# The sign of a float64 weight through a leaky rectifier and a shift, and a new order for the kernel's head

## The chip, the cores and the metric

The kernel runs on one core of a Trainium2 chip. A core has a matrix engine (TensorE, PE in the profile, with its weight loads as PEld), a vector engine (VectorE, DVE), an activation engine (ScalarE, ACT), a general engine (GpSimd, POOL), and a queue engine (SyncE, SP) that here issues all transfers. Each engine takes its instructions strictly in the program's order and waits on semaphores for the others. The metric is the device time of one execution in microseconds (us), median of three runs; lower is better.

## The reference

Three stages follow each other over 4,608 tokens of 512 values (8 batches x 576 positions; 8 heads x 64):

```
q_s = softmax(q, over the 64 of a head);  k_s = softmax(k, over the 576 positions)
x   = q_s @ (k_s^T v)                      # linear attention, heads side by side
g   = silu(x @ w_in);  x2 = g @ w_out      # 512 -> 2048 -> 512
logits = x2 @ phi                          # 32 slots
d = softmax(logits, over tokens);  slots = d^T x2
so = relu(slots @ w1) @ w2, by expert      # 8 experts, 4 slots each
out = softmax(logits, over slots) @ so
```

`w_in` and `w_out` reach the chip as float64, so the kernel must make float32 of their two 32-bit words itself.

## The kernel before, in words

The tokens go through in 18 chunks of 256 (`c`). For a chunk, `qs` is the softmax of q, `qT` its transposition and split into a rounded high part and a rest (`qhi`, `qlo`), `x` the attention product with its own split, `h.c.s` (s = 0 to 7) 24 matmuls with one eighth of `w_in` (`win_hi[s]`, `win_lo[s]`, into one of three PSUM buffers), followed by tanh on ACT, a product on DVE (`u`) and a 32x32 transposition (`gT`). `l`, `dl`, `ds`, `dT` make logits and the running softmax over tokens. `rg` regroups `gT` by 16 transfers into `gk` and `dg` multiplies it with the softmax (the product `sg`). The attention matrices come from 16 units (`u`, half a batch each): `km` maximum, `kT` its transposition, whose maximum `mt` is split (`mh`) and multiplied into a diagonal `dg` tile, `ks` subtraction, `ke` exponential, `kv` matmul and normalisation (`kvtmp`, `kvn_hi`, `kvn_lo`).

No scheduler decides the order. Three strings, START, CHUNK and END, list steps by name; `play` (end of the kernel) runs the next piece of the named generator each time that a name comes up, and every engine gets its instructions in that order. A `*` behind a name puts the step's `combine2` (line 161, a product or a difference of two tiles) on DVE instead of POOL. START makes chunks 0 and 1 and, among them, converts the 16 float64 pieces that the head needs: `w.0` to `w.7` (eighths of `w_in`, each then split into `win_hi` and `win_lo`) and `p.0` to `p.7` (eighths of `w_out`, multiplied with phi into `wphi`). CHUNK, played for chunks 2 to 14, converts `w_out` once more in 16 half pieces (`o`), which are stored to DRAM for the end.

A conversion (`to_f32`) takes, for each piece of 128 x 1024 values: on ACT the high word scaled by 2^-112 (line 384), and the sign of the high word, written over it (line 385); on DVE a left shift by 3 (line 387) and the low word's top bits or-ed in (line 388); on POOL, as a rule, the product with the sign (line 161). The raw words lie in buffers that are loaded again when the piece has been read for the last time, and the raw pieces `p.6` and `p.7` lie in the buffer that `rg.0` writes next. Converted pieces (`mg`) have three buffers.

Of the kernel before, what the change touches and what calls it, by code (L numbers as in the profile page):

```python
# [20 lines left out]


START = """
lq.0 lk.0.0 qs.0 qs.0 qs.0 qs.0 km.0 kT.0 qs.0 kT.0 kT.0 qs.0 lk.1.0 lw.0 km.1 qs.0 ks.0 kT.1 qs.0 w.0 ks.0
qs.0 kT.1 ke.0 qT.0.0 kT.1 lw.1 ks.1 qT.0.0 qT.0.0 w.1 w.0 w.0 ks.1 lphi lk.0.1 lk.1.1 lw.2 kv.0 qT.0.1 ke.1
w.1 w.0 lq.1 kv.1 w.2 qT.0.1 w.1 kv.0 w.0* qs.1 qT.0.1 w.1 kv.0 lw.3 lk.3.0 w.1 w.2 qs.1 lw.4 qs.1 kv.0 kv.1
w.2 kv.1 w.3 kv.1 km.3 kT.3 w.3 x.0.0 qs.1 w.2 x.0.1 x.0.0 w.4 w.3 w.2 x.0.1 kT.3 kT.3* x.0.0 lw.5 qs.1 w.3
w.4 lp.0 w.5 x.0.1 ks.3 qs.1 w.4 h.0.0 ks.3 w.3 w.5 h.0.1 qs.1 w.4 h.0.0 h.0.0 qs.1 w.4* w.5 h.0.2 qs.1 p.0
h.0.1 w.5 lp.1 lk.3.1 p.1 h.0.2 ke.3 lw.6 p.0 h.0.3 w.5 qT.1.0 h.0.1 h.0.4 p.0 lw.7 p.0 p.1 h.0.2 w.6 w.6 p.1
lp.2 qT.1.0 w.7 h.0.4 h.0.3 p.0 w.7 kv.3 p.1 h.0.5 qT.1.0 w.6 p.0 x.1.0 w.6 p.1 qT.1.1 p.1 h.0.3 h.0.4 p.0 p.1  # L30
w.7 kv.3 w.6* h.0.5 qT.1.1 w.7 x.1.0 l.0.1 h.0.6 lk.2.0 p.2 km.2 qT.1.1 x.1.0 p.2 kT.2 w.7 h.0.5 h.0.7 x.1.1
lp.3 p.2 kT.2 kT.2 p.2 kv.3 h.0.6 p.3 h.0.7 x.1.1 p.3 x.1.1 h.0.6 p.2 lp.4 lk.2.1 p.2 h.1.0 ks.2 p.4 lp.5 lq.2
h.0.7 kv.3 p.3 p.3 lp.6 p.4 p.5 p.3 h.1.0 p.4 p.5 h.1.1 p.3 h.1.2 qs.2 p.2 p.4 qs.2 ks.2 p.6 p.4 lp.7 p.3 qs.2
p.5 ke.2 l.0.3 p.4 h.1.0 p.5 h.1.1 p.5 p.7 qs.2 p.6 h.1.3 h.1.2 qs.2 h.1.3 p.6 h.1.1 p.4 p.7 p.5 kv.2 kv.2
p.7* h.1.4 p.6 p.5 qs.2 p.6* h.1.2 p.7 l.0.5 qs.2 p.6 h.1.5 qs.2 qs.2 p.7* kv.2 h.1.4 h.1.3 p.6 rg.0 p.7 h.1.6
p.7 qT.2.0 l.0.7 kv.2 h.1.4 h.1.5 qT.2.0 rg.0 qT.2.0 x.2.0 dl.0 x.2.0 dl.0 qT.2.1 h.1.5 rg.0 qT.2.1 qT.2.1
h.1.7 ds.0 ds.0 x.2.0 ds.0 x.2.1 l.1.1 dT.0 l.1.3 rg.0 x.2.1 h.1.7 h.1.6 dT.0 x.2.1 h.1.6 dg.0 dg.0 h.1.7 lq.3
lk.4.0 lk.4.1 l.1.5
"""
# [24 lines left out]
def kernel(  # L64
# [330 lines left out]
    def conv_w(j):
        yield from to_f32(("w", j), cv_p)
        yield
        t = c_t.pop(("w", j))
# [544 lines left out]
```

## Time and profile before

| | |
|---|---|
| median of three runs (lowest, highest) | 743.89 us (743.63 to 743.97) |
| span of the profiled execution, first to last instruction | 741.5 us |
| busy in that span: PE, DVE, ACT, POOL | 674.9, 569.3, 285.7, 154.2 us |
| mean granted TensorE clock (1 is 2.4 GHz) | 0.970 |

The profile gives the profiled execution's span; the runs' times hold in addition what lies around it, 743.89 - 741.5 = 2.4 us at the median. A busy time is a sum over a program whose stages have different limits, so it is read by stage. A clock of 0.5 in a stretch means 1.2 GHz, 1.0 means 2.4 GHz.

### The profile page before, as it was taken

Reading aid. Unit: us, or ns where it says so; the run is one execution under the profiler, and the core shown is the slowest. Engines: PE = TensorE matmul, PEld = TensorE weight load, DVE = VectorE, ACT = ScalarE, POOL = GpSimd, SP = SyncE. Lnnn points to the kernel's source line nnn. Section 1 sums busy time; section 2 is a strip of 40 time slices with the busy share of each in tenths; the row PEclk is TensorE's granted clock in tenths of the full one; section 3 lists DMA queues with packets and bytes.
Section 4 is the critical chain, followed back from the end, with each engine's and each line's share of the span. In section 5 each row is a group of like instructions: output and inputs, shape, how many; then the busy total and the mean of one; then the engine's idle time right before and its main releaser. Section 6 shows DMA issues by size and latency. Waiting matters only on the chain.

```text
span 741.5 us, 15214 instructions
## 1 busy us (share of the span) xinstructions
PE 674.9 (91%) x6214; PEld 574.7 (77%) x6214; DVE 569.3 (77%) x998; ACT 285.7 (39%) x512; POOL 154.2 (21%) x108
## 2 busy tenths in 40 slices
PE   1347699999999999999999999999999999998993
PEld 1247588889897987989798898989898998893452
DVE  8999999788887979798888778878896784334253
ACT  3466564233444344333434334242433323322223
POOL 4857564011202111122112111010201000003000
PEclk9759799999999999999999999999999999999998
DMA  8623733665565739374765626845351747799998
GB/s 344 276 108 114 304 138 79 187 192 122 161 151 168 199 117 234 99 223 96 204 158 170 143 60 183 264 136 129 102 114 41 217 93 242 265 357 374 369 374 340
DMA packets 39509, 141.73 MB, mean 191 GB/s; under 512 B 6672, under 2 KB 6672, under 8 KB 30736
## 3 DMA queue, kind: packets, MB, share of 16 engines
q1 hardware_dynamic: 39440, 140.76, 60.4%
q8 instruction: 49, 0.80, 0.5%
q14 instruction: 20, 0.16, 0.1%
HBM read 93.55 MB, written 13.63 MB: 145 GB/s over the span
## 4 chain that ended last, share of the span: by engine, by line
PE 71%; DVE 17%; SPq 3%; issue 3%; ACT 2%; DMA 2%; POOL 0%; DVEq 0%; POOLq 0%; ACTq 0%
PE h L432 45%; PE sg L554 5%; PE pl L481 5%; SPq L491 3%; PE l L833 2%; DMA gk<-gT 2%; PE l L806 2%; PE kv L241 2%; DVE mg_p L388 2%; DVE mg_w L388 1%; PE x L348 1%; PE x L349 1%; DVE u L445 1%; PE x L347 1%; PE po L855 1%
## 5 line engine op out<-in xcount | busy, mean ns | idle before, releaser
L432 PE MATMUL h<-x,win_hi 128*128 128x256 f32 x2304 | 432.4, 289 | 5.0 <-DVE u L445 4.1
L432 PEld LDWEIGHTS h<-x,win_hi 128*128 128x128 f32 x2304 | 362.3, 194 | 32.7 <-issue 30.4
L432 PE MATMUL h<-x,win_lo 128*128 128x256 f32 x1152 | 328.1, 285 | 2.0 <-DVE win_lo L161 2.0
L432 PEld LDWEIGHTS h<-x,win_lo 128*128 128x128 f32 x1152 | 222.9, 193 | 2.3 <-DVE win_lo L161 2.3
L443 ACT ACTIVATE u<-h 128x512 f32<-128x512 f32 x144 | 85.5, 596 | 181.6 <-PE h L432 175.7
L445 DVE SCALAR_TENSOR_TENSOR u<-u,h 128x512 f32<-128x512 f32 x144 | 97.1, 674 | 51.0 <-ACT u L443 50.9
L452 DVE STREAM_TRANSPOSE gT<-u 128x512 f32<-128x512 f32 x128 | 91.1, 712 | 4.5
L161 POOL TENSOR_TENSOR q<-q,qsm 128x1024 f32<-128x1024 f32 x16 | 31.6, 1977 | 173.0 <-DVE qsm L303 76.8
L481 PE MATMUL pl<-u,wphi 128*32 128x256 f32 x576 | 47.5, 394 | 2.7 <-DVE wphi L419 2.7
L554 PE MATMUL sg<-gk,d 128*32 128x512 f32 x288 | 40.5, 594 | 1.8 <-DMA gk<-gT 1.4
L354 DVE TENSOR_TENSOR x<-x,x 128x512 fp32r<-128x512 f32 x36 | 24.7, 686 | 22.0 <-ACT x L352 21.5
L161 POOL TENSOR_TENSOR qlo<-q,qhi 128x512 fp32r<-128x512 f32 x17 | 22.5, 1322 | 90.6 <-ACT qhi L329 90.6
L294 ACT ACTIVATE q<-q 128x1024 f32<-128x1024 f32 x18 | 19.1, 1060 | 52.9 <-DVE q L161 48.9
L193 DVE TENSOR_REDUCE m<-kv 128x256 f32<-128x1280 f32 x16 | 39.3, 2454 | 0.0
L352 ACT CAST x<-x 128x512 fp32r<-128x512 f32 x36 | 21.0, 584 | 42.5 <-PE x L349 42.2
L161 POOL TENSOR_TENSOR mg_o<-mg_o,raw_o 128x512 f32<-128x512 f32 x16 | 20.9, 1308 | 73.3 <-DVE mg_o L388 64.8
L257 ACT CAST kvn_hi<-kvtmp 64x128 fp32r<-64x128 f32 x32 | 9.5, 296 | 51.2 <-DVE kvtmp L252 50.8
L329 ACT CAST qhi<-q 128x512 fp32r<-128x512 f32 x34 | 20.9, 615 | 18.9 <-DVE q L323 13.3
L348 PE MATMUL x<-qlo,kvn_hi 128*128 128x256 f32 (+3 forms) x96 | 27.3, 285 | 0.0
L349 PE MATMUL x<-qhi,kvn_lo 128*128 128x256 f32 (+3 forms) x96 | 27.2, 284 | 0.0
L347 PE MATMUL x<-qhi,kvn_hi 128*128 128x256 f32 (+3 forms) x96 | 27.2, 283 | 0.0
L554 PEld LDWEIGHTS sg<-gk,d 128*32 128x32 f32 x288 | 12.1, 109 | 18.7 <-issue 11.8
(155 smaller groups left out, 905.6 us busy)
## 6 DMA issues: line engine op xcount, KB each, us to landing
gk<-gT SPq DMA_DIRECT2D x256, 128.0 KB, 2.5
w<-in_moe_w_dram SPq DMA_DIRECT2D x32, 1024.0 KB, 7.5
kv<-in_kv_dram SPq DMA_DIRECT2D x16, 650.0 KB, 6.2
kv<-in_kv_dram SPq DMA_DIRECT2D x16, 640.0 KB, 4.9
q<-in_q_dram SPq DMA_DIRECT2D x18, 512.0 KB, 3.5
raw_w<-in_moe_w_in_dram SPq DMA_DIRECT2D x8, 1024.0 KB, 7.4
raw_p<-in_moe_w_out_t_dram SPq DMA_DIRECT2D x8, 1024.0 KB, 7.9
raw_o<-in_moe_w_out_dram SPq DMA_DIRECT2D x8, 1024.0 KB, 6.9
```

The lines of the kernel that those rows point to most:

```text
L161: (nc.vector if star[0] else nc.gpsimd).tensor_tensor(*a)
L193: nc.vector.tensor_reduce(m1.rearrange("p (h d) -> p h d", h=HH), k_t[u].rearrange("p h j d -> p h d j"), axis=AX.X, op=ALU.max,)
L347: nc.tensor.matmul(o, kh, qh[:, i, p0:p1], start=True, stop=False)
L348: nc.tensor.matmul(o, kh, ql[:, i, p0:p1], start=False, stop=False)
L349: nc.tensor.matmul(o, kl, qh[:, i, p0:p1], start=False, stop=True)
L354: nc.vector.tensor_tensor(lo, px, hi.bitcast(F32), ALU.subtract)
L432: nc.tensor.matmul(ph[:, i, :], a, x[:, kk, :], start=(n == 0), stop=(n == 3 * KD - 1))
L443: nc.scalar.activation(u, ph, AF.Tanh, scale=0.5)
L445: nc.vector.scalar_tensor_tensor(u, u, 1.0, ph, ALU.add, ALU.mult)
L452: nc.vector.transpose(out=gT_t[c][:, :, 2 * s:2 * s + 2, :].rearrange("p j a f -> p a j f"), in_=u.rearrange("p a (j t) -> p a j t", t=32),)
L481: nc.tensor.matmul(pl_t[c][NS * g:NS * g + NS, :], wphi[:, ft, :], u[:, i, :], start=(ft < G), stop=(ft >= KF - G))
L554: nc.tensor.matmul(pg[NS * i:NS * i + NS, :], d[:, j, :], gk[:, j, i, :], start=(j == 0), stop=(j == TPC - 1))
```

## The change

Sign and product go away. A leaky rectifier (Prelu) passes positive inputs and multiplies negative ones with alpha, here -2^32: the result is positive for both, and for a negative input its exponent is larger by 32, a bit that the left shift by 3 moves to the place of the sign. The piece of a generator that held the product is gone, so each `w`, `p` and `o` has a step less (for `o` two). START is written anew: the loads, conversions and chunk steps of the head come in another order, with other steps marked by `*`. CHUNK only loses two of its six `o`. END is the same.

```
-lq.0 lk.0.0 qs.0 qs.0 qs.0 qs.0 km.0 kT.0 qs.0 kT.0 kT.0 qs.0 lk.1.0 lw.0 km.1 qs.0 ks.0 kT.1 qs.0 w.0 ks.0
+lq.0 lk.0.0 lw.0 lk.1.0 qs.0 qs.0 lk.0.1 lw.2 qs.0 km.0 qs.0 lw.3 w.0 w.0 kT.0 qs.0 qs.0 qs.0 kT.0 qs.0 lw.1
...
-            nc.scalar.activation(mg[:, a], top, AF.Copy, scale=2.0 ** -112)
-            nc.scalar.activation(top, top, AF.Sign)
+            nc.scalar.activation(mg[:, a], top, AF.Prelu, scale=2.0 ** -112, alpha=-2.0 ** 32)
             yield
             nc.vector.tensor_scalar(m, m, 3, None, ALU.logical_shift_left)
             nc.vector.scalar_tensor_tensor(m, w[:, a, :, 0], 29, m, ALU.logical_shift_right, ALU.bitwise_or)
-            yield
-            combine2(mg[:, a], mg[:, a], top, ALU.mult)
             if i < cuts - 1:
                 yield
```

What the new order does is read from the engines' instruction lists. Line numbers behind `to_f32` are four lower after the change, those ahead of it one lower. A number directly behind a tile's name is its piece, unit or chunk; the last number is a buffer's. First POOL in the early head, from the first conversions on, before:

```order
L161 TENSOR_TENSOR qlo0_0_244<-qt0_0_245,qhi0_0_243 128x512
L161 TENSOR_TENSOR mg_w0_232<-mg_w0_232,raw_w0_218 128x1024
L161 TENSOR_TENSOR mg_w1_258<-mg_w1_258,raw_w0_218 128x1024
L161 TENSOR_TENSOR qlo0_1_292<-qt0_1_293,qhi0_1_291 128x512
L161 TENSOR_TENSOR win_lo1_151<-mg_w1_258,win_hi1_143 128x1024
L161 TENSOR_TENSOR mg_w2_322<-mg_w2_322,raw_w2_268 128x1024
L161 TENSOR_TENSOR q1_299<-q1_299,qmx1_333 128x1024
L161 TENSOR_TENSOR mg_w3_360<-mg_w3_360,raw_w2_268 128x1024
L161 TENSOR_TENSOR win_lo2_152<-mg_w2_322,win_hi2_144 128x1024
L161 TENSOR_TENSOR mg_w4_391<-mg_w4_391,raw_w4_347 128x1024
L161 TENSOR_TENSOR win_lo3_153<-mg_w3_360,win_hi3_145 128x1024
```

and after, up to the last `win_lo`:

```order
L160 TENSOR_TENSOR win_lo0_150<-mg_w0_208,win_hi0_142 128x1024
L160 TENSOR_TENSOR qlo0_1_267<-qt0_1_268,qhi0_1_266 128x512
L160 TENSOR_TENSOR win_lo2_152<-mg_w2_235,win_hi2_144 128x1024
L160 TENSOR_TENSOR q1_306<-q1_306,qmx1_308 128x1024
L160 TENSOR_TENSOR win_lo4_154<-mg_w4_424,win_hi4_146 128x1024
L160 TENSOR_TENSOR q1_306<-q1_306,qsm1_493 128x1024
L160 TENSOR_TENSOR win_lo5_155<-mg_w5_427,win_hi5_147 128x1024
L160 TENSOR_TENSOR qlo1_0_542<-q1_306,qhi1_0_541 128x512
L160 TENSOR_TENSOR win_lo6_156<-mg_w6_545,win_hi6_148 128x1024
```

The products `mg_w...<-mg_w...,raw_w...` are gone, and from POOL's list up to the `dg2` tile six `win_lo` differences stand there instead of five, and one `qlo` less. Next DVE, from the maximum of unit 3 to the second half of chunk 0's x, before:

```order
L193 TENSOR_REDUCE m1_3_365<-kv3_340 128x256
L387 TENSOR_SCALAR mg_w3_360<-mg_w3_360 128x1024
L388 SCALAR_TENSOR_TENSOR mg_w3_360<-raw_w2_268,mg_w3_360 128x1024
L207 TENSOR_REDUCE mt3_397<-m1T_10_367 128x2
L209 CAST mh3_399<-mt3_397 128x2
L210 TENSOR_TENSOR mt3_397<-mt3_397,mh3_399 128x2
L161 TENSOR_TENSOR dg3_402<-ident_74,mh3_399 128x128 x2
L161 TENSOR_TENSOR dg3_402<-ident_74,mt3_397 128x128 x2
L354 TENSOR_TENSOR x1_0_373<-x_11_374,x0_0_372 128x512
L387 TENSOR_SCALAR mg_w4_391<-mg_w4_391 128x1024
L388 SCALAR_TENSOR_TENSOR mg_w4_391<-raw_w4_347,mg_w4_391 128x1024
L354 TENSOR_TENSOR x1_0_373<-x_12_383,x0_0_372 128x512
```

and after:

```order
L192 TENSOR_REDUCE m1_3_349<-kv3_311 128x256
L353 TENSOR_TENSOR x1_0_352<-x_10_353,x0_0_351 128x512
L206 TENSOR_REDUCE mt3_372<-m1T_11_365 128x2
L208 CAST mh3_374<-mt3_372 128x2
L209 TENSOR_TENSOR mt3_372<-mt3_372,mh3_374 128x2
L259 TENSOR_TENSOR kvn_lo0_160<-kvtmp1_346,kvn_hi0_158 64x2x64 x2
L385 TENSOR_SCALAR mg_w3_362<-mg_w3_362 128x1024
L386 SCALAR_TENSOR_TENSOR mg_w3_362<-raw_w2_201,mg_w3_362 128x1024
L353 TENSOR_TENSOR x1_0_352<-x_12_387,x0_0_351 128x512
L160 TENSOR_TENSOR win_lo1_151<-mg_w1_247,win_hi1_143 128x1024
L160 TENSOR_TENSOR win_lo3_153<-mg_w3_362,win_hi3_145 128x1024
L160 TENSOR_TENSOR dg3_430<-ident_74,mh3_374 128x128 x2
```

Before, five conversions (`mg_w0` to `mg_w4`) and the `dg3` tile stand ahead of the second x1_0 row; now four conversions do, and `dg3`, `mg_w4` and two `win_lo` follow it. `win_lo0`, which stood further ahead on DVE, is on POOL now. Last DVE, at the end of the conversions, before (`mg_p6`, then `mg_p7` with its product on DVE):

```order
L387 TENSOR_SCALAR mg_p6_955<-mg_p6_955 128x1024
L388 SCALAR_TENSOR_TENSOR mg_p6_955<-raw_p6_877,mg_p6_955 128x1024
L445 SCALAR_TENSOR_TENSOR u1_1_980<-u1_1_980,h1_1_891 128x512
L452 STREAM_TRANSPOSE gT1_973<-u1_1_980 128x2x8x32
L419 TENSOR_SCALAR wphi_87<-wphi_30_969 128x64
L387 TENSOR_SCALAR mg_p7_984<-mg_p7_984 128x1024
L388 SCALAR_TENSOR_TENSOR mg_p7_984<-raw_p6_877,mg_p7_984 128x1024
L249 TENSOR_SCALAR rz2_1050<-kv_33_1029 128x2
L250 RECIPROCAL rz2_1050<-rz2_1050 128x2
L252 TENSOR_TENSOR kvtmp2_1053<-kv_33_1029,rz2_1050 128x128
L161 TENSOR_TENSOR mg_p7_984<-mg_p7_984,raw_p6_877 128x1024
```

and after, where `mg_p7` comes first and `mg_p6` later:

```order
L385 TENSOR_SCALAR mg_p7_983<-mg_p7_983 128x1024
L386 SCALAR_TENSOR_TENSOR mg_p7_983<-raw_p6_793,mg_p7_983 128x1024
L296 TENSOR_REDUCE qsm2_989<-q2_789 128x32
L224 TENSOR_TENSOR kv2_683<-kv2_683,mb_29_977 128x5x4x64
L248 TENSOR_SCALAR rz3_996<-kv_16_595 128x2
L249 RECIPROCAL rz3_996<-rz3_996 128x2
L251 TENSOR_TENSOR kvtmp3_999<-kv_16_595,rz3_996 128x128
L385 TENSOR_SCALAR mg_p6_909<-mg_p6_909 128x1024
L386 SCALAR_TENSOR_TENSOR mg_p6_909<-raw_p6_793,mg_p6_909 128x1024
L301 SCALAR_TENSOR_TENSOR qsm2_989<-qsm2_989,qsm_31_1029 128x32
L302 RECIPROCAL qsm2_989<-qsm2_989 128x32
L415 TENSOR_SCALAR wphi_87<-wphi_30_1026 128x64
```

Behind `mg_p6` DVE goes on with the q product of chunk 2 (`q2_789<-q2_789,qsm2_989`, on POOL before), a fifth u of chunk 1, a `qlo` of chunk 2 and the second `kvn_lo` of batch 1. Up to that `kvn_lo` (unit 2's, the last that x of chunk 2 needs) DVE's list holds, before: `win_lo0`, `win_lo4`, `win_lo6` and the product of `mg_p7`, and 12 u; after: `win_lo1`, `win_lo3`, the q product, two `qlo`, and 13 u. All else up to there is the same work in another order. On ACT the whole program has one load of the function tables before and one after; in the head after, the 16 Prelu stand in nine groups between instructions that use Exp or Tanh.

## Rows read from the trace of the kernel before

**Rows 1.** Busy us by engine in four stretches, with clock, DMA share and GB/s.

```profile
0.00:49.81 49.81, 13.16 (x110) 10.73 (x111) 44.90 (x68) 24.76 (x28) 31.02 (x30) 0.82 0.68 271
49.81:88.89 39.08, 28.33 (x228) 25.31 (x227) 38.60 (x38) 24.02 (x30) 28.08 (x12) 0.81 0.42 158
88.89:140.64 51.75, 50.74 (x459) 43.72 (x459) 45.51 (x70) 25.07 (x37) 21.80 (x13) 0.96 0.49 157
140.64:640.00 499.36, 495.78 (x4596) 440.20 (x4596) 402.51 (x740) 182.26 (x349) 65.99 (x46) 1.00 0.57 155
```

**Rows 2.** DVE's groups up to 128.3 us: busy us, mean ns | idle before.

```profile
L388 DVE SCALAR_TENSOR_TENSOR mg_w<-raw_w,mg_w 128x1024 uint32<-128x1024 uint32 x8 | 15.0, 1872 | 0.3
L388 DVE SCALAR_TENSOR_TENSOR mg_p<-raw_p,mg_p 128x1024 uint32<-128x1024 uint32 x8 | 14.0, 1754 | 0.3
L387 DVE TENSOR_SCALAR mg_p<-mg_p 128x1024 uint32<-128x1024 uint32 x8 | 9.6, 1203 | 0.0
L452 DVE STREAM_TRANSPOSE gT<-u 128x512 f32<-128x512 f32 x12 | 8.5, 711 | 0.5
L387 DVE TENSOR_SCALAR mg_w<-mg_w 128x1024 uint32<-128x1024 uint32 x8 | 9.1, 1140 | 0.0
L161 DVE TENSOR_TENSOR win_lo<-mg_w,win_hi 128x1024 fp32r<-128x1024 f32 x3 | 8.4, 2804 | 0.0
L445 DVE SCALAR_TENSOR_TENSOR u<-u,h 128x512 f32<-128x512 f32 x12 | 8.0, 667 | 0.0
L209 DVE CAST mh<-mt 128x2 fp32r<-128x2 f32 x4 | 3.7, 916 | 0.1
L161 DVE TENSOR_TENSOR mg_p<-mg_p,raw_p 128x1024 f32<-128x1024 f32 x1 | 1.2, 1215 | 0.0
```

**Rows 3.** DVE's instructions in order of time: start us, us, engine, line, what.

```profile
11.10 0.17 DVE L209 CAST mh<-mt 128x2 fp32r<-128x2 f32 x1
...
44.07 2.20 DVE L209 CAST mh<-mt 128x2 fp32r<-128x2 f32 x1
46.31 2.27 DVE L210 TENSOR_TENSOR mt<-mt,mh 128x2 f32<-128x2 f32 x1
...
91.65 0.68 DVE L387 TENSOR_SCALAR mg_p<-mg_p 128x1024 uint32<-128x1024 uint32 x1
92.37 1.22 DVE L388 SCALAR_TENSOR_TENSOR mg_p<-raw_p,mg_p 128x1024 uint32<-128x1024 uint32 x1
...
127.71 0.56 DVE L260 TENSOR_TENSOR kvn_lo<-kvtmp,kvn_hi 64x128 fp32r<-64x128 f32 x2
```

**Rows 4.** POOL's instructions in order of time, around 45 us.

```profile
43.84 2.41 POOL L161 TENSOR_TENSOR mg_w<-mg_w,raw_w 128x1024 f32<-128x1024 f32 x1 [4.88 <-issue]
46.20 2.35 POOL L161 TENSOR_TENSOR win_lo<-mg_w,win_hi 128x1024 fp32r<-128x1024 f32 x1
```

**Rows 5.** POOL's groups up to 128.3 us.

```profile
L161 POOL TENSOR_TENSOR mg_w<-mg_w,raw_w 128x1024 f32<-128x1024 f32 x8 | 19.6, 2456 | 16.0 <-issue 6.1 <-DVE mg_w L388 4.5 <-ACT raw_w L385 3.4
L161 POOL TENSOR_TENSOR mg_p<-mg_p,raw_p 128x1024 f32<-128x1024 f32 x7 | 17.3, 2478 | 15.3 <-issue 7.9 <-DVE mg_p L388 4.6 <-ACT u L443 2.8
L161 POOL TENSOR_TENSOR win_lo<-mg_w,win_hi 128x1024 fp32r<-128x1024 f32 x5 | 12.8, 2559 | 0.0
```

**Rows 6.** ACT's groups up to 128.3 us.

```profile
L384 ACT ACTIVATE mg_w<-raw_w 128x1024 f32<-128x1024 f32 x8 | 9.2, 1155 | 5.4 <-issue 4.8 <-POOL win_lo L161 0.5
L294 ACT ACT_TABLE_LOAD x1 | 1.3, 1283 | 4.3 <-DMA q<-in_q_dram 4.3
```

**Rows 7.** The chain that ended last, around 135 us: start us, us, what.

```profile
130.43 0.23 PE x L347
...
140.64 4.39 PE h L432 x35
```

**Rows 8.** PE's instructions in order of time: the first of h.

```profile
49.81 0.81 PE L432 MATMUL h<-x,win_hi 128*128 128x256 f32 x2
```

**Rows 9.** SP's instructions in order of time: chunk 0's regrouping.

```profile
121.23 10.43 SPq L491 DMA_DIRECT2D gk<-gT  x16
```

More of the change, by code (lines that the diff above doesn't have):

```diff
@@ L23 @@
 START = """
-lq.0 lk.0.0 qs.0 qs.0 qs.0 qs.0 km.0 kT.0 qs.0 kT.0 kT.0 qs.0 lk.1.0 lw.0 km.1 qs.0 ks.0 kT.1 qs.0 w.0 ks.0
[L25 to L38, printed above, removed]
+lq.0 lk.0.0 lw.0 lk.1.0 qs.0 qs.0 lk.0.1 lw.2 qs.0 km.0 qs.0 lw.3 w.0 w.0 kT.0 qs.0 qs.0 qs.0 kT.0 qs.0 lw.1
@@ new lines @@
+km.1 kT.0 w.2 ks.0 kT.1 qs.0 lphi w.2 w.1 kT.1 w.0 lk.1.1 ks.0 kT.1 qT.0.0 qT.0.1 ke.0 ks.1 qT.0.0 ks.1 ke.1
+kv.0 w.1 kv.0 w.0 lq.1 qs.1 qT.0.1 lk.3.0 kv.1 qs.1 lw.4 kv.0 kv.0 qT.0.0* kv.1 qs.1 km.3 x.0.0 w.2 x.0.0 w.3
+x.0.0 kT.3 kv.1 qT.0.1 w.2 kT.3 kv.1 qs.1 lk.3.1 lw.5 lp.0 w.3 lp.1 x.0.1 x.0.1 x.0.1 w.1 w.1* w.3 h.0.0 w.4
+w.3* w.5 qs.1 kT.3* h.0.0 w.4 h.0.1 p.0 w.5 h.0.2 qs.1 h.0.1 qs.1 qs.1 h.0.0 lw.6 w.4 w.4 h.0.1 w.5 qs.1 w.5
+ks.3 h.0.3 qT.1.0 ks.3 w.6 p.0 h.0.4 p.1 p.1 lw.7 h.0.4 w.6 ke.3 p.0 h.0.3 h.0.2 p.0 kv.3 qT.1.0 h.0.2 w.7 lp.2
@@ new lines @@
+w.6 p.1 qT.1.0 w.7 w.6 p.0 p.1 w.7 h.0.5 h.0.3 h.0.4 h.0.5 x.1.0 x.1.0 p.1 lk.2.0 w.7 h.0.6 qT.1.1 p.2 h.0.7
+qT.1.1 km.2 h.0.6 lp.3 p.3 lp.4 x.1.0 p.0 qT.1.1 x.1.1 p.2 p.1 h.0.5 lp.5 x.1.1 x.1.1 p.3 p.2 h.0.6 p.2 p.5 p.4
+l.0.1 lq.2 h.0.7 lp.6 kT.2 h.1.0 h.0.7 p.5 h.1.2 p.4 h.1.1 h.1.0 kT.2 p.3 p.2 p.4 h.1.1 qs.2 p.3 p.2 lp.7 h.1.2
+p.6 p.3 h.1.0 qs.2 qs.2 kT.2 h.1.1 h.1.3 h.1.6 ks.2 h.1.2 p.3 p.7 qs.2 qs.2 p.7 qs.2 ks.2 h.1.6 p.4 kv.3 h.1.4
+p.4 qs.2 lk.2.1 ke.2 p.6 qs.2 l.0.3 p.5 h.1.4 p.4 p.5 kv.3 p.6 p.7 qs.2* p.5 p.6* h.1.4 kv.2 kv.3 p.6 rg.0 p.6
@@ L39 @@
+rg.0 h.1.3 p.7* h.1.5 qT.2.0 lk.4.0 kv.2 rg.0 p.5 p.7 kv.2 l.0.5 qT.2.0 h.1.3 qT.2.0* p.7 lk.4.1 l.0.7 kv.2 dl.0
+dl.0 x.2.0 x.2.0 qT.2.1 ds.0 ds.0 qT.2.1 h.1.7 qT.2.1 x.2.1 ds.0 h.1.6 x.2.0 dT.0 h.1.5 l.1.1 dT.0 x.2.1 h.1.5
+h.1.7 l.1.3 h.1.7 l.1.5 rg.0 x.2.1 dg.0 lq.3 dg.0
 """
 CHUNK = """
-qs rg km h.0 h.0 o h.1 qs e.7 rg h.1 dl kT o h.0 kT sc sc kT* dl qs qs* h.1 h.2 rg ks ds h.3 ks ds qs h.2 h.3
-ds sc ke h.4 dT qs sc h.2 dT qs ol qs h.3 rg kv l.1 dg kv o sc qs qT.0 h.5 kv ow qT.0 h.4 kv qT.0* h.4 x.0 h.5
@@ L43 @@
-o qT.1 h.5 qT.1 x.0 qT.1 l.3 h.6 x.1 h.7 l.5 lk dg x.0 o x.1 h.6 x.1 h.6 o h.7 h.7 lq
+qs rg km h.0 h.0 o h.1 qs e.7 rg h.1 dl kT o h.0 kT sc sc kT* dl qs qs* h.1 h.2 rg ks ds h.3 ks ds qs h.2 h.3 ds
+sc ke h.4 dT qs sc h.2 dT qs ol qs h.3 rg kv l.1 dg kv sc qs qT.0 h.5 kv ow qT.0 h.4 kv qT.0* h.4 x.0 h.5 o qT.1
+h.5 qT.1 x.0 qT.1 l.3 h.6 x.1 h.7 l.5 lk dg x.0 o x.1 h.6 x.1 h.6 h.7 h.7 lq
 """
```

## The prediction

> **What bounds the kernel now.** I read the busy time by stretch first [rows 1]. From 140.64 to 640 us PE is busy 495.78 of 499.36 us at full clock: there the matmuls bound the kernel, and what DVE, ACT or POOL save is hidden. The head is another matter. In its first two stretches PE is busy 13.16 of 49.81 us and 28.33 of 39.08 us at clocks of 0.82 and 0.81, while DVE is busy 44.90 and 38.60 us, nearly without a gap. From 88.89 to 140.64 us PE is busy 50.74 of 51.75 us. So DVE bounds the kernel up to about 89 us, and PE then works off what DVE has delivered late. ACT (about half busy) and POOL bound nothing by themselves.
>
> The second view is DVE's own time. A conversion's or-instruction takes 1.22 us when nothing disturbs it and its shift 0.68 us [rows 3], but their means up to 128 us are 1.75 to 1.87 and 1.14 to 1.20 us [rows 2]. Why, two pairs show: a cast of 128 x 2 values takes 0.17 us at 11.10 us and 2.20 us at 44.07 us, and the tiny subtraction behind it 2.27 us [rows 3]. Each ends within 0.05 us of a POOL instruction, a sign product (43.84 + 2.41) and a `win_lo` difference (46.20 + 2.35) [rows 4]. DVE stands still until POOL's instruction is over, and the profile counts that as busy.
>
> These stalls, summed over the groups of [rows 2] as mean minus undisturbed time: or-instructions 8 x 0.65 + 8 x 0.53 = 9.5 us, shifts 8 x 0.46 + 8 x 0.52 = 7.9 us, three `win_lo` on DVE 3 x (2.80 - 1.22) = 4.8 us, four casts 4 x (0.92 - 0.17) = 3.0 us: 25.2 us of the first 128. They are the cover under which this head is slow.
>
> **The change, part by part.** *Sign on ACT.* Sixteen instructions fall away in the head and sixteen shorter ones in the chunk loop, in the head about the size of the copy that stays, 1.16 us [rows 6], so some 18 us of ACT. ACT is half busy and not on the chain; I cost this at nothing. Cover: DVE's list in the head, PE in the loop. Prelu itself stands in no row. Nearest is the scaled copy of the same tile, 1.16 us; the other end is that each change of function costs a table load of 1.28 us more [rows 6]. I take the copy's price, since the program has one load as before; the other end is a rival below.
>
> *Products on POOL.* Fifteen go from the head, 19.6 + 17.3 = 36.9 us of POOL's 80.9 us up to 140.6 us [rows 1, 5]. POOL's own time is off the path; what counts is the stalls that they cause on DVE. The sixteenth stood on DVE (1.22 us [rows 2]). In the chunk loop sixteen shorter products go, under PE's cover: worth nothing, or at most part of the 3.6 us that PE idles there [rows 1]. If that cover were gone, DVE would be stalled there the same way.
>
> *The new order, on DVE.* The last thing that x of chunk 2 waits for is the `kvn_lo` of unit 2, which ends at 127.71 + 0.56 = 128.3 us [rows 3]. Ahead of it after the change: one u more (0.67 + 0.71), two `win_lo` (2 x 1.22), the q product (1.22, the same size), two `qlo` of half that size (estimate 2 x 0.61); in all 6.3 us. No longer ahead of it: three `win_lo` and a product, 4 x 1.22 = 4.9 us [rows 2]. Net +1.4 us.
>
> *The stalls that stay.* POOL keeps 80.9 - 36.9 = 44 us, less a little, in it six `win_lo` of 2.4 to 2.6 us [rows 4, 5]. Before, 80.9 us of POOL cost DVE 25.2 us, 0.31 us each us; at that rate 44 us cost 13.6. The lower end is 3 us (a `win_lo` or two that meet a conversion), the upper 44 us (each blocks DVE for all its length). I take 7 us, half the rate: in the new list the last four `win_lo` and the `qlo` meet DVE mostly at u, transpositions and reductions, whose means, 0.67 us for u and 0.71 for gT, show no such stretching [rows 2].
>
> *New waits.* With the stalls gone DVE meets others that are not ready. Its list puts the sum behind unit q1 ahead of u0_0, and that sum's matmul stands on PE behind h0_2; ACT does u0_2 only behind u0_4, kv3 and u0_3, so h0_5 waits for its PSUM buffer. Before, DVE's gaps in the head are small (49.81 - 44.90 = 4.9 us, then 0.5 [rows 1]). Bounds for more: 0 and 9 us (three h of about 3 us); I take 3.
>
> *The sum.* 128.3 - 25.2 + 1.4 + 7 + 3 = 114.5 us for that `kvn_lo`. From x of chunk 2 to the first h of chunk 2 PE took 140.64 - 130.43 = 10.2 us [rows 7], the same matmuls after the change. So h of chunk 2 starts at 124.8 us instead of 140.64: 15.8 us earlier. From there the program is the same and bound by PE. The span goes from 741.5 to 725.7 us, and the time, with the 2.4 us around it, to 743.9 - 15.8 = **728 us**.
>
> *Can PE keep up?* h starts at 49.81 us [rows 8]. Ahead of it on DVE go at least the two stalls of [rows 4] (4.1 us), one conversion (1.9), and a `win_lo` with its stall (2.8): 8.8 us. From 49.81 to 140.64 us PE idles 10.75 + 1.01 = 11.8 us [rows 1]. Without both, and at the same clocks, h of chunk 2 could start at 140.6 - 8.8 - 11.8 = 120 us. That is a floor close under 124.8; less time at 1.2 GHz would lower it by a few us.
>
> **The rule on the port.** The row: DVE's 0.17 us cast takes 2.20 us and ends with POOL's product [rows 3, 4]. The Trainium skill, page "SBUF — State Buffer", section "Who interferes with whom", says that DVE and GpSimd share a port pair as an exclusive lock: the second to start blocks until the first has finished, if DVE's instruction is of a fast two-port kind or reads two SBUF operands. The trace agrees as far as the pairs show. Taken at its strictest, for every POOL instruction that is left, it gives the second rival.
>
> **Rivals.**
> *New waits take most of it.* The order is tight: u, PSUM buffers, regrouping. Chunk 0's regrouping is the clearest place: its 16 transfers were issued from 121.23 us for 10.43 us [rows 9], when piece p.7 was done, and now wait for the late p.6, about 6 us ahead of the `kvn_lo`, at 108 us; their last lands near 121, just ahead of the products that need it. If DVE waits 9 us and the rate of 13.6 us holds, the `kvn_lo` ends at 127 and the time is 741; half of that again would leave no change. For it: DVE becomes one of three nearly equal chains. Against: PE's floor is 120.
>
> *Slower: what is left on POOL blocks DVE fully.* Place: the six `win_lo`, the q differences and `qlo`, on DVE's list. Price: up to 44 us instead of 7, time up to 743.9 - 15.8 + 37 = 765. It decides from 23 us of stalls. Against: 81 us of POOL cost only 25.
>
> *Slower: Prelu is of another table.* Nine groups of Prelu among Exp and Tanh would mean 18 loads of 1.28 us, 23 us on ACT; if all lie on the path, 751 us; it turns slower from 13 of them. The Trainium skill, page "ScalarE: Activation LUTs", section "Table sets: the hidden batching unit", names relu and copy among the functions that every set has, not Prelu; no run here shows it. Against: the program loads once.
>
> *Larger gain.* Stalls of 3 us, no waits, and a clock that rises earlier: 119 us or less for h of chunk 2, time 717 to 722.
>
> **How the numbers follow.** My forecast (stalls and waits between 4 and 17 us together, 722 to 735): 0.72. New waits: 0.12, of it 0.09 for 735 to 742 and 0.03 for no change. Full blocking 0.04, tables 0.02. Larger gain 0.10. The range is 717 to 738: it takes in the larger gain and the first part of the new waits, and leaves out some 0.13 above. Within 0.2% (1.5 us) is about what a measurement of this kernel can't tell from no change; faster has 0.72 + 0.09 + 0.10 = 0.91, same 0.03, slower 0.06.
>
> **What would show it.** Right: `mg` shifts and or-instructions near 0.68 and 1.22 us on DVE, long ones only beside `win_lo` or q instructions on POOL; the first h near 40 us; h of chunk 2 near 125; from there the same distance to the end; Prelu near 1.16 us and one table load. Wrong: or-instructions that still take 1.8 us; gaps on DVE that name PE, ACT or a transfer for over 10 us together; PE idle in front of the products `sg` of chunk 0; more idle time on PE in the loop than 3.6 us.

## The result and the profile after

The changed kernel takes **714.0 us** (median of 4 runs, 712.8 to 716.5) beside 743.9 for the kernel before, measured along with it: a ratio of 0.960, 95% interval 0.957 to 0.963. It gained 29.9 us where I had forecast 15.8, and it lies 3 us below my range. The profiled execution took 714.5 us, its span 712.7.

The busy time by stretch, to be read beside [rows 1] (columns: stretch, length, then busy us of PE, weight loads, DVE, ACT and POOL, clock, DMA share, GB/s; the cuts are just behind the first h at 35.06 us, at 65 us, and just behind the start of h of chunk 2 at 114.62 us):

```profile
0.00:35.26 35.26, 13.41 (x109) 10.34 (x110) 31.40 (x64) 13.80 (x17) 18.28 (x25) 0.94 0.83 326
35.26:65.00 29.74, 27.16 (x247) 25.48 (x246) 28.45 (x37) 21.73 (x28) 14.53 (x7) 0.95 0.66 250
65.00:114.69 49.69, 47.71 (x443) 40.01 (x441) 41.04 (x77) 19.25 (x34) 5.07 (x7) 0.97 0.57 178
114.69:612.00 497.31, 496.01 (x4604) 441.33 (x4605) 404.82 (x739) 171.89 (x333) 45.05 (x30) 1.00 0.58 157
```

The first h starts at 35.1 us instead of 49.8 [rows 8], h of chunk 2 at 114.6 instead of 140.6, and from 35.26 us up to there PE is busy 74.9 of 79.4 us. Behind it PE is busy 496.0 of 497.3 us, so the chunk loop is bound by PE as before. So 26 of the 30 us were won in the head.

DVE's groups up to the end of the last `kvn_lo` of unit 2, now at 102.8 us (mean ns behind the comma; the first five groups answer to lines of [rows 2]):

```profile
L386 DVE SCALAR_TENSOR_TENSOR mg_w<-raw_w,mg_w 128x1024 uint32<-128x1024 uint32 x8 | 9.8, 1226 | 0.3
L386 DVE SCALAR_TENSOR_TENSOR mg_p<-raw_p,mg_p 128x1024 uint32<-128x1024 uint32 x8 | 9.8, 1225 | 0.3
L385 DVE TENSOR_SCALAR mg_w<-mg_w 128x1024 uint32<-128x1024 uint32 x8 | 6.5, 809 | 0.9 <-ACT mg_w L383 0.9
L385 DVE TENSOR_SCALAR mg_p<-mg_p 128x1024 uint32<-128x1024 uint32 x8 | 5.4, 676 | 0.0
L208 DVE CAST mh<-mt 128x2 fp32r<-128x2 f32 x4 | 0.7, 169 | 0.1
L209 DVE TENSOR_TENSOR mt<-mt,mh 128x2 f32<-128x2 f32 x4 | 0.6, 160 | 0.1
L259 DVE TENSOR_TENSOR kvn_lo<-kvtmp,kvn_hi 64x128 fp32r<-64x128 f32 x8 | 2.2, 277 | 0.1
L192 DVE TENSOR_REDUCE m<-kv 128x256 f32<-128x1280 f32 x4 | 9.5, 2381 | 0.0
```

None of these is stretched any more, except two shifts by 0.5 us each (they make the mean 809). Yet POOL keeps six `win_lo` of 2.4 to 3.4 us. Where they went, two lists in order of time show, POOL and then DVE:

```profile
28.18 2.76 POOL L160 TENSOR_TENSOR win_lo<-mg_w,win_hi 128x1024 fp32r<-128x1024 f32 x1 [1.26 <-ACT win_hi L395]
...
48.29 2.42 POOL L160 TENSOR_TENSOR win_lo<-mg_w,win_hi 128x1024 fp32r<-128x1024 f32 x1
```

```profile
29.39 2.41 DVE L192 TENSOR_REDUCE m<-kv 128x256 f32<-128x1280 f32 x1
...
47.98 0.71 DVE L448 STREAM_TRANSPOSE gT<-u 128x512 f32<-128x512 f32 x1
48.62 0.67 DVE L322 STREAM_TRANSPOSE q<-q 128x512 f32<-128x512 f32 x1
49.21 1.45 DVE L224 TENSOR_TENSOR kv<-kv,mb 128x1280 f32<-128x1280 f32 x1
```

Beside a `win_lo` DVE now works on a maximum, on transpositions, or on something that it reads from PSUM (`mb`, `h`), and these keep their times: the transposition of u 0.71 us as in the kernel before [rows 2], the maximum 2.38 us in the mean, where before it took 2.36:

```profile
L193 DVE TENSOR_REDUCE m<-kv 128x256 f32<-128x1280 f32 x4 | 9.4, 2362 | 0.0
```

On PE, x of chunk 2 starts where that `kvn_lo` ends, and the regrouped pieces of chunk 0 are the last thing waited for ahead of h of chunk 2:

```profile
102.91 0.30 PE L346 MATMUL x<-qhi,kvn_hi 128*128 128x64 f32 x1
...
112.81 1.88 PE L550 MATMUL sg<-gk,d 128*32 128x512 f32 x10 [0.76 <-DMA gk<-gT]
114.62 0.50 PE L428 MATMUL h<-x,win_hi 128*128 128x256 f32 x2
```

Prelu takes the time of the scaled copy [rows 6], and one table is loaded, at 0.7 us:

```profile
L383 ACT ACT_TABLE_LOAD x1 | 1.3, 1283 | 0.7 <-PEq L928 0.7
...
L383 ACT ACTIVATE mg_w<-raw_w 128x1024 f32<-128x1024 f32 x8 | 9.1, 1155 | 18.0 <-DMA raw_w<-in_moe_w_in_dram 18.0
```

### The profile page after: what moved, and what is told of

Read it like the earlier page. It is cut to its first block, busy times and chain, and to the rows that moved or that the text cites. A ratio compares the mean times of both kernels' runs of the same rounds, so it can differ in the third digit from the quotient of the medians.

```text
span 712.7 us, 15115 instructions
## 1 busy us (share of the span) xinstructions
PE 671.3 (94%) x6214; PEld 572.1 (80%) x6214; DVE 543.0 (76%) x999; ACT 256.0 (36%) x480; POOL 90.2 (13%) x75
## 4 chain that ended last, share of the span: by engine, by line
PE 78%; DVE 9%; DMA 5%; SPq 3%; ACT 2%; issue 2%; DVEq 0%; ACTq 0%
PE h L428 51%; PE sg L550 5%; PE pl L477 5%; SPq L487 3%; DMA gk<-gT 2%; PE l L829 2%; PE kv L240 2%; PE l L802 2%; PE po L851 2%; DMA raw_p<-in_moe_w_out_t_dram 2%; PE x L348 1%; PE x L347 1%; PE x L346 1%; PE uT L461 1%; DMA raw_w<-in_moe_w_in_dram 1%
## 5 line engine op out<-in xcount | busy, mean ns | idle before, releaser
L160 POOL TENSOR_TENSOR q<-q,qsm 128x1024 f32<-128x1024 f32 x15 | 28.7, 1914 | 259.9 <-DVE qsm L302 188.2
L477 PE MATMUL pl<-u,wphi 128*32 128x256 f32 x576 | 46.0, 390 | 0.3 <-DVE wphi L415 0.3
L160 POOL TENSOR_TENSOR qlo<-q,qhi 128x512 fp32r<-128x512 f32 x16 | 20.7, 1296 | 105.1 <-ACT qhi L328 105.1
L240 PE MATMUL kv<-kv 128*64 128x65 f32 x640 | 24.0, 235 | 3.3 <-ACT kv L231 3.3
L550 PEld LDWEIGHTS sg<-gk,d 128*32 128x32 f32 x288 | 11.8, 109 | 18.7 <-issue 13.0
L322 DVE STREAM_TRANSPOSE q<-q 128x512 f32<-128x512 f32 x34 | 23.5, 692 | 3.8 <-POOL q L160 3.8
```

What stands on the lines that cost most here:

```text
L240: nc.tensor.matmul(pk[D * e:D * e + D, i, :], kt[:, 2 * i + e, j, :], va[:, 2 * i + e, j, :], start=(j == 0), stop=(j == KJ - 1),)
L477: nc.tensor.matmul(pl_t[c][NS * g:NS * g + NS, :], wphi[:, ft, :], u[:, i, :], start=(ft < G), stop=(ft >= KF - G))
L550: nc.tensor.matmul(pg[NS * i:NS * i + NS, :], d[:, j, :], gk[:, j, i, :], start=(j == 0), stop=(j == TPC - 1))
```

## The experiments

Theory A: DVE's stalls beside POOL's work made the head slow; without products, and with the rest of POOL's work placed beside DVE work that it doesn't stall, they are gone. Theory B: the new order, with its earlier loads, brings the time, whatever POOL does. Theory C: the arithmetic alone brings it.

For each run I summed the **stalls**: DVE's conversions, casts, `mt`, `win_lo`, `kvn_lo` and q steps up to the last `kvn_lo` of unit 2, each one's duration less its undisturbed one (or-instruction 1.22 us, shift 0.68, cast 0.17, `mt` 0.16, `win_lo` 1.22, `kvn_lo` 0.28, q product 1.22, `qlo` 0.69); and DVE's **waits** there, as the trace names them. Ratios are to the kernel before, measured along with each. The time is a median; the last four columns are of the one run that was profiled, whose time stands ahead of them and can lie some us from the median.

| kernel | time us | ratio (95%) | profiled run us | first h | stalls | waits | last `kvn_lo` ends |
|---|---|---|---|---|---|---|---|
| before | 743.9 | 1 | 743.9 | 49.8 | 29.9 | 4.9 | 128.3 |
| changed | 714.0 | 0.960 (0.957 to 0.963) | 714.5 | 35.1 | 1.1 | 7.0 | 102.8 |
| arithmetic alone | 730.6 | 0.983 (0.981 to 0.986) | 727.8 | 43.1 | 14.1 | 8.9 | 115.2 |
| order alone | 746.3 | 1.006 (1.003 to 1.008) | 746.1 | 41.1 | 24.8 | 15.1 | 135.9 |
| idle products | 734.8 | 0.988 (0.985 to 0.991) | 730.6 | 39.7 | 18.7 | 6.7 | 120.8 |
| idle copies | 726.1 | 0.977 (0.974 to 0.979) | 725.7 | 39.9 | 11.6 | 5.3 | 112.9 |
| Sign kept | 720.6 | 0.971 (0.968 to 0.973) | 723.1 | 36.1 | 2.2 | 11.2 | 109.4 |
| arithmetic alone, Sign kept | 730.6 | 0.984 (0.981 to 0.988) | 730.2 | 45.0 | 14.2 | 9.7 | 117.0 |
| loop as before | 714.2 | 0.962 (0.959 to 0.964) | 715.1 | 34.9 | 1.0 | 4.9 | 101.3 |
| no or-instructions | 708.5 | 0.953 (0.950 to 0.956) | 708.2 | 34.8 | 0.5 | 21.9 | 98.8 |

### The two parts of the change

Arithmetic alone (the old lists without the product steps):

```diff
-            nc.scalar.activation(mg[:, a], top, AF.Copy, scale=2.0 ** -112)
-            nc.scalar.activation(top, top, AF.Sign)
+            nc.scalar.activation(mg[:, a], top, AF.Prelu, scale=2.0 ** -112, alpha=-2.0 ** 32)
...
-            yield
-            combine2(mg[:, a], mg[:, a], top, ALU.mult)
```

> The rectifier and the shift carry the sign, but all steps stay in the order of before; the product steps are dropped from it. Theory A (DVE loses its time standing still beside POOL's two-input instructions; the products are half of them, and the new order keeps the rest away from DVE's SBUF work): the stalls that win_lo causes stay, those of the products go, so about half to two thirds of the 30 us gained: 722 to 729 us, mean of the or-instruction on DVE up to the end of the head between 1.3 and 1.6 us. Theory B (the new order, with earlier loads and another sequence, brings it; the arithmetic only shortens ACT and POOL, which bound nothing): 738 to 744 us. Theory C (the arithmetic alone brings it all, the order nothing): 713 to 717 us.

Order alone (the new lists; the product follows in the step of the or-instruction):

```diff
             nc.vector.scalar_tensor_tensor(m, w[:, a, :, 0], 29, m, ALU.logical_shift_right, ALU.bitwise_or)
-            yield
             combine2(mg[:, a], mg[:, a], top, ALU.mult)
```

> The new order with the arithmetic of before (scaled copy, Sign, and the product on POOL right behind the or-instruction). Theory A: fifteen products of 2.4 us are back beside DVE, so the or-instructions and shifts are long again, 15 to 25 us of stalls: 728 to 742 us. Theory B: 714 to 720 us, since POOL and ACT have room. Theory C: 738 us or more, the order alone gives nothing.

730.6 and 746.3 us: neither part does it, and their effects (by the ratios some 13 us gained and some 4 lost) don't add up to 29.9. Theories B and C are out. Theory A's own ranges were missed as well, 722 to 729 by 1.6 us and 728 to 742 by 4.3; the marks that it named came, or-instructions of 1.49 us with the arithmetic alone (1.3 to 1.6 expected) and stalls of 24.8 us with the order alone (15 to 25). DVE's conversions with the arithmetic alone, up to 115.2 us:

```profile
L387 DVE SCALAR_TENSOR_TENSOR mg_p<-raw_p,mg_p 128x1024 uint32<-128x1024 uint32 x8 | 12.0, 1496 | 0.3
L387 DVE SCALAR_TENSOR_TENSOR mg_w<-raw_w,mg_w 128x1024 uint32<-128x1024 uint32 x8 | 11.9, 1490 | 0.3
L386 DVE TENSOR_SCALAR mg_w<-mg_w 128x1024 uint32<-128x1024 uint32 x8 | 9.2, 1154 | 0.0
```

Two groups with the order alone, up to 135.9 us:

```profile
L387 DVE SCALAR_TENSOR_TENSOR mg_w<-raw_w,mg_w 128x1024 uint32<-128x1024 uint32 x8 | 15.0, 1870 | 0.3
L208 DVE CAST mh<-mt 128x2 fp32r<-128x2 f32 x4 | 5.4, 1357 | 0.1
```

Without products the old order keeps 14.1 us of stalls, from `win_lo` and q steps that meet conversions. With products the new order keeps 24.8 us, and DVE waits 15.1 us besides, so that it is slower than before. Together they leave 1.1 us.

### Does POOL's work itself do it?

Into the changed kernel I put one more POOL instruction behind each of the head's sixteen conversions. It writes to the logits' tile, which is free then. First a product, then a copy:

```diff
+            if key[0] != "o":
+                spare = logit[:, 0:32, :].rearrange("p (a t) s -> p a (t s)", a=n)
+                nc.gpsimd.tensor_tensor(spare, mg[:, a], mg[:, a], ALU.mult)
```

> The changed kernel, with one 128x1024 product more on POOL behind each of the sixteen conversions of the head; it reads the converted piece twice and writes into the logits' tile, which is free then, and nobody waits for its values. It leaves nothing of the computation out. Theory A (POOL's two-input work itself stalls DVE): 8 to 20 us slower than the changed kernel, 722 to 734 us, with or-instructions and shifts of 1.4 us or more in the mean. Theory B (the products cost by the chain conversion, product, win_hi, and by the order): 714 to 718 us, means near 1.23 and 0.75 us; some of it could come from win_lo, which queue behind the products on POOL.

```diff
-                nc.gpsimd.tensor_tensor(spare, mg[:, a], mg[:, a], ALU.mult)
+                nc.gpsimd.tensor_copy(spare, mg[:, a])
```

> As the run with idle products (734.8 us), but the sixteen instructions on POOL are copies of the same 128x1024 tiles, one input instead of two. If any work of POOL on SBUF stalls DVE: 728 to 736 us, or-instructions near 1.75 us again. If what stalls DVE is an instruction with two inputs: 714 to 719 us and or-instructions near 1.23 us; some of it could then be win_lo and q steps that queue behind the copies.

The products cost 20.8 us, above my bound of 20, and stalls rise by 17.6. The copies cost 12.1 us, with 10.5 us more of stalls; their 726.1 us lie in neither of the two ranges, so the guess that only two inputs on POOL count fell, and so did the one that any instruction there costs the same. A tiny cast, beside a product and beside a copy (DVE and POOL in order of time):

```profile
95.23 1.89 POOL L389 TENSOR_TENSOR logit<-mg_p 128x1024 f32<-128x1024 f32 x1 [1.23 <-DVE mg_p L386]
95.46 1.69 DVE L208 CAST mh<-mt 128x2 fp32r<-128x2 f32 x1
```

```profile
88.90 1.04 POOL L389 COPY logit<-mg_p 128x1024 f32<-128x1024 f32 x1 [1.20 <-DVE mg_p L386]
89.14 0.83 DVE L208 CAST mh<-mt 128x2 fp32r<-128x2 f32 x1
```

Each time the 0.17 us cast ends with POOL's instruction: the shorter instruction costs less, no more. The or-instructions' mean was 1.74 us with products and 1.40 with copies, the shifts' 0.79 and 0.83, where I had expected 1.4 or more for both with products. Part of either cost is that `win_lo` and the q steps queue behind the added instruction and then meet conversions.

### Sign and the chunk loop

Sign put back on ACT, its values unused, in the changed kernel and in the old order with the new arithmetic:

```diff
             nc.scalar.activation(mg[:, a], top, AF.Prelu, scale=2.0 ** -112, alpha=-2.0 ** 32)
+            nc.scalar.activation(top, top, AF.Sign)
```

> The changed kernel, with the Sign activation of before put back on ACT behind each rectifier, its values used by nobody: ACT works as long as before. If ACT's time is free, as I costed it: 714 to 716 us. Rival (part of the gain that I did not forecast comes from a shorter ACT, which delivers u and win_hi earlier): 718 to 724 us, with DVE waits that name ACT for 4 us or more in the head.

> The kernel with the rectifier in the order of before (arith alone, 730.6 us), with the Sign put back on ACT, its values used by nobody. If ACT is free in that order, as it looked in the profile of before: 729 to 732 us, and the 13 us that the arithmetic alone gained are all the products'. If ACT's time counts there as it did in the new order (6 to 7 us there): 735 to 740 us, and only some 6 us are the products'.

In the old order it costs nothing that can be told: 730.6 us with and without it. In the new one it costs 6.6 us (720.6; by the two ratios, 8). The stretch from 35 to 65 us, of the changed kernel and then with Sign (columns as in the first view):

```profile
35.00:65.00 30.00, 27.41 (x248) 25.74 (x247) 28.71 (x37) 21.73 (x28) 14.53 (x7) 0.95 0.66 252
```

```profile
35.00:65.00 30.00, 24.80 (x195) 22.81 (x196) 25.50 (x34) 25.03 (x29) 8.66 (x5) 0.78 0.56 211
```

ACT is busy 25.0 of 30 us, and DVE 3.2 us less than without Sign. PE's clock has a mean of 0.78 instead of 0.95: from 55 to 60 us PE is busy 1.3 of 5 us (5.0 without Sign), and from 60 to 65 us the clock is 0.50, that is 1.2 GHz (1.00 without). DVE's waits that name ACT come to 4.9 us up to the last `kvn_lo`, 2.5 in the changed kernel. The longest of DVE's waits with Sign (us in total, times, longest), and POOL's list:

```profile
DVE x L353 <- ACT x L351: 2.7, 2, 2.4
DVE q L322 <- POOL q L160: 2.5, 1, 2.5
DVE u L442 <- ACT u L440: 1.4, 1, 1.4
```

```profile
48.55 2.41 POOL L160 TENSOR_TENSOR win_lo<-mg_w,win_hi 128x1024 fp32r<-128x1024 f32 x1 [14.68 <-ACT win_hi L396]
50.92 1.92 POOL L160 TENSOR_TENSOR q<-q,qsm 128x1024 f32<-128x1024 f32 x1
```

ACT's late `win_hi` holds POOL; the q product behind it starts at 50.9 us, and in the changed kernel at 46.4:

```profile
46.42 1.91 POOL L160 TENSOR_TENSOR q<-q,qsm 128x1024 f32<-128x1024 f32 x1
```

DVE waits 2.5 us for it.

In the chunk loop, the conversion and list of before (head as changed):

```diff
+            if key[0] == "o":
+                nc.scalar.activation(mg[:, a], top, AF.Copy, scale=2.0 ** -112)
+                nc.scalar.activation(top, top, AF.Sign)
...
+                combine2(mg[:, a], mg[:, a], top, ALU.mult)
```

> The changed kernel, but the sixteen half pieces of w_out in the chunk loop are converted as before, with Sign and product, and the loop's list is that of before; the head is that of the change. Theory A (the products and Signs of the loop, which I costed at nothing, held the chunk loop up by some 3 us): 716 to 719 us, and the time from the first sg to the end of the span 2 us or more longer. Theory B (PE covers them, as forecast; the loop's few us come from elsewhere, such as late transfers): 713 to 715.5 us, the same distance within 1 us.

714.2 us, ratio 0.962 (0.959 to 0.964): by the time, the loop's products and Signs cost nothing that can be told. The second mark, though, fell on theory A's side: from the first `sg` to the end of the span it took 604.3 us, 2.2 more than in the changed kernel (602.1). This distance varies: it is 604.2 with Sign kept, and over all fourteen profiles 599.9 to 604.3. So a cost of up to some 2 us in the loop isn't excluded.

### What bounds the changed kernel

> The changed kernel without the sixteen or-instructions of the head (it leaves out the low three bits of each mantissa of w and p), to see what bounds the changed kernel now: 16 x 1.23 = 19.6 us less on DVE, 3.7 us of it ahead of the first h. If DVE's list still sets the end of the head alone: the last kvn_lo near 84 us and a time near 695 us. If PE does from the first h on (27.2 of 29.7 and 47.7 of 49.7 us busy): only the three or-instructions ahead of the first h and the 4.6 us of idle PE behind it can be had, 705 to 710 us. If transfers or ACT do: 711 to 714 us.

```diff
-            nc.vector.scalar_tensor_tensor(m, w[:, a, :, 0], 29, m, ALU.logical_shift_right, ALU.bitwise_or)
+            if key[0] == "o":
+                nc.vector.scalar_tensor_tensor(m, w[:, a, :, 0], 29, m, ALU.logical_shift_right, ALU.bitwise_or)
```

This kernel leaves out the low three mantissa bits of w and p. 19.6 us less on DVE bring 5.5 us (708.5): DVE now waits 21.9 us, and PE is full:

```profile
65.00:90.00 25.00, 25.00 (x229) 23.05 (x231) 17.51 (x34) 11.54 (x16) 3.39 (x5) 1.00 0.59 198
```

So, behind the first h, the changed head is within some 6 us of what PE allows. Four tries to start h earlier found nothing. The zeros of the kvn tiles on ACT:

```diff
-        nc.gpsimd.memset(t.bitcast(F32), 0.0)
+        for i in range(NPAIR):
+            nc.scalar.activation(t[:, i, :], ident, AF.Copy, scale=0.0)
```

> The changed kernel with the zeros of the four kvn tiles written by ACT (sixteen scaled copies of 128x128 by 0, while ACT waits for its first piece of w) instead of four memsets on POOL, beside which DVE's first copies stand still for up to 1.7 us. If those stalls are POOL's: the copies of the set-up end at 3.8 to 4.0 us in place of 4.4 to 5.3, and 712 to 714 us, at most 1.5 us better, about what the measurement can tell. If DVE then waits for the first q or for ACT: no difference, 713 to 716 us.

The maximum over the K of unit 3 behind x of chunk 0, in two ways, and the second with those zeros too (the lists' places):

```diff
-kv.0 w.1 kv.0 w.0 lq.1 qs.1 qT.0.1 lk.3.0 kv.1 qs.1 lw.4 kv.0 kv.0 qT.0.0* kv.1 qs.1 km.3 x.0.0 w.2 x.0.0 w.3
-x.0.0 kT.3 kv.1 qT.0.1 w.2 kT.3 kv.1 qs.1 lk.3.1 lw.5 lp.0 w.3 lp.1 x.0.1 x.0.1 x.0.1 w.1 w.1* w.3 h.0.0 w.4
+kv.0 w.1 kv.0 w.0 lq.1 qs.1 qT.0.1 lk.3.0 kv.1 qs.1 lw.4 kv.0 kv.0 qT.0.0* kv.1 qs.1 x.0.0 x.0.0 kv.1 w.2
+x.0.0 qT.0.1 w.2 kv.1 qs.1 w.3 km.3 kT.3 lk.3.1 lw.5 lp.0 x.0.1 x.0.1 x.0.1 w.3 kT.3 lp.1 w.1 w.1* w.3 h.0.0 w.4
...
+x.0.0 kv.1 qT.0.1 w.2 kv.1 qs.1 lk.3.1 lw.5 lp.0 w.3 lp.1 x.0.1 x.0.1 x.0.1 km.3 w.1 w.1* w.3 h.0.0 kT.3 w.4
```

> The changed kernel with another order at one place: the 2.4 us maximum over the K of unit 3 and what follows it, which stand on DVE ahead of the last kvn_lo and x of chunk 0, go behind them, and two conversions of w with them. If the first h of chunk 0 (35.06 us) sets what comes after, since PE is busy 27.2 of 29.7 us from there on: the first h 1.5 to 2.5 us earlier and 711 to 713 us. If the DVE list up to 103 us sets it, whatever the order in it: 713 to 716 us, no difference.

> The maximum over the K of unit 3 moved again, since in the run before (716.2 us) its transposition stood on PE ahead of x of chunk 0 and made it wait 4.4 us: now the maximum goes behind x of chunk 0 on DVE and its transposition behind the first h on PE. If the first h sets what follows: the first h 1.5 to 2.5 us earlier, near 33 us, and 711 to 713 us. If what is lost by the late unit 3 or by ACT takes it back: 713.5 to 716 us.

> The same order, and the zeros of the kvn tiles written by ACT: the set-up ends 0.7 to 1.6 us earlier. If both gains come through to the first h: near 32.5 us and 710 to 712.5 us. If the head is held elsewhere: 713 to 716 us.

713.8, 716.2, 716.6 and 716.0 us, with ratios from 0.959 to 0.964: none can be told from the change, and 716.2 and 716.6 lie just above both of their ranges. The first h came at 34.7, 35.6, 34.4 and 34.5 us. The zeros on ACT did end the set-up at 3.9 us in place of 5.5 (or 4.7), but the first h came only 0.4 us earlier than in the changed kernel. In the first of the two orders my edit left the maximum's transposition on PE ahead of x, which waited 4.4 us for it. In the second the maximum no longer lay beside POOL's `win_lo` and the q step behind it, and something that stalls did (POOL, then DVE):

```profile
28.24 2.75 POOL L160 TENSOR_TENSOR win_lo<-mg_w,win_hi 128x1024 fp32r<-128x1024 f32 x1 [1.26 <-ACT win_hi L395]
30.95 1.91 POOL L160 TENSOR_TENSOR q<-q,qmx 128x1024 f32<-128x1024 f32 x1
```

```profile
31.55 1.78 DVE L259 TENSOR_TENSOR kvn_lo<-kvtmp,kvn_hi 64x128 fp32r<-64x128 f32 x2 [0.52 <-ACT kvn_hi L256]
```

The two `kvn_lo` that take 0.6 us undisturbed took 1.8: in the changed kernel the 2.4 us maximum covers them.

## Why the prediction was wrong

The forecast of 728 us is 14 us above the measured time. Some 10 of them lie ahead of h of chunk 2 (124.8 us forecast, 114.6 measured), 4 behind it.

**The mechanism was right.** DVE's stalls beside POOL's work were the head's cost, the products were what to remove, and the time is gained ahead of h of chunk 2. Products that nobody needs bring the stalls back. But without the products the old order gains only 13 of the 30 us; the new order, whose effect on the stalls I had put at half the rate, is what takes the rest of POOL's work out of DVE's way.

**The step that failed** is "The stalls that stay": 7 us, measured 1.1. I took half of a mean rate per us of POOL. There is no such rate: what a `win_lo` costs depends on which DVE instruction is due beside it, and I could have read that from the new list. Without the products POOL is busy 41.0 us up to the last `kvn_lo` in the old order and 36.6 in the new one; DVE's stalls there are 14.1 us, near the full rate's 13.6, and 1.1. The Trainium skill, page "SBUF — State Buffer", section "Who interferes with whom", says that a DVE reduction never contends on trn2, and that an instruction with one SBUF input outside the two-port modes doesn't either. The trace agrees: the maximum took 2.36 us before and 2.38 after, the transposition 0.71 in both. I quoted the lock and not this half of it.

**The stalls were undercounted.** My 25.2 us left out `mt` (4 x 0.53 = 2.1 us) and `kvn_lo` (8 x 0.33 = 2.7 us). With both corrections the sum goes from 114.5 to 114.5 - 5.9 - 4.8 = 103.8. The waits were 2.1 us more than before, not 3, and the set-up ended 0.9 us earlier, by chance (see the last section): 103.8 - 0.9 - 0.9 = 102.0, beside 102.8 measured. That chance didn't make the gain: the run with the loop as before has the same head, its set-up ended late, at 5.5 us, and its last `kvn_lo` at 101.3.

**Sign at nothing** held only for the old order (0.0 us); in the new one the Signs cost 6.6. I costed each part with the others' cover as it was before; with DVE no longer late, ACT is close to being late.

**PE's floor at 120 us** was wrong too: h of chunk 2 starts at 114.6. I let the first h come 8.8 us earlier, it came 14.7, and I kept the clocks of 0.82 and 0.81, where the changed kernel had 0.94 to 0.97. From the first h to h of chunk 2 PE idles 4.6 us instead of 11.8, and the distance falls from 90.8 to 79.6 us. The matmuls between are the same (686 in the trace after, 685 in that before), so some 4 us of it are the clock's. My rival "Larger gain" named an earlier clock and stalls of 3 us; it came nearest, with a chance of 0.10, and its 717 us were still too many.

**Right by their sizes:** the new waits (2.1 for 3, a guess between 0 and 9), Prelu at the copy's price with one table, chunk 0's regrouping as the last wait, at 0.8 us, the loop's products at nothing, within some 2 us. From x to h of chunk 2 PE took 11.7 us instead of 10.2 [rows 7] for the same matmuls, 0.8 of the difference by that wait.

**Open.** After h of chunk 2, 4 us more were gained (29.9 less 26.0): 0.6 of them lie around the span, 0.5 are the profiled run's distance from the median, and 2.8 lie behind h of chunk 2. From the first to the last start of `sg` it took 534.3 us before and 532.3 after, but 530.5 with the order alone, which has all the products and Signs, and 534.5 with the loop as before. PE's waits in that stretch show part of it: 0 to 3.4 us for regrouping transfers (`gk`), which differ from profile to profile without a link to the change, and 1.1 us once for a `dg` tile of DVE, in the kernel before and in the one with the loop as before, and in none of the other twelve. So about 1 us may be the loop's old list with its products; for the rest I have no cause.

## What to carry to other kernels

Before moving or dropping work on POOL, list what DVE does beside each POOL instruction. In these traces maxima (2.4 us), transpositions (0.7) and work that reads from PSUM (u, 0.67) kept their times, while shifts, casts (0.17 us, up to 2.20), or-instructions (1.22 us, 1.87 in the mean) and differences of two SBUF tiles stood still until POOL was done. Place the first kind beside POOL, and don't price the rest by a mean rate. When two edits each remove a cover from the other, test them together: here one alone gained 13 us, the other lost 4, and both gained 30. After a large gain, ask again what each "free" engine costs.

## What was not expected of the hardware

A copy with one input on POOL (1.04 us) holds DVE until it ends, just as a product does. POOL gives way too: a `win_lo` takes 2.4 us undisturbed, and where the first of two started 0.1 us behind an or-instruction of DVE (58.27 us), they took 5.74 together, while the or-instruction kept its 1.23:

```profile
58.40 5.74 POOL L160 TENSOR_TENSOR win_lo<-mg_w,win_hi 128x1024 fp32r<-128x1024 f32 x2 [0.71 <-ACT win_hi L395]
```

At the start, DVE's first copies meet POOL's memsets, and how they share differs between executions. In ten of the twelve profiles that have these memsets (the lines below are of Sign kept; DVE, then POOL) DVE stood until the memsets were over, and in two, the changed kernel's among them, the copies took 0.67 us and each pair of memsets 1.11; the set-up then ended 0.9 us earlier:

```profile
1.33 2.07 DVE L708 COPY s<-ident 32x32 f32<-32x32 f32 x4 [1.33 <-POOL ident masks.py:199]
```

```profile
1.39 0.99 POOL L704 MEMSET kvn_hi<- 128x512 f32 x2
2.32 0.99 POOL L704 MEMSET kvn_lo<- 128x512 f32 x2
```
